# A fused attention and feed-forward kernel: the third tile of p, divided by its sums ahead, is transposed by DMA in 27 of 36 units, in a new order of all engines' steps

## The chip, the cores and the metric

One Trainium2 chip, one NeuronCore. The metric is the device time of one execution in microseconds. Engines: PE (TensorE, matrix products), DVE (VectorE), ACT (ScalarE), POOL (GpSimd), SP (SyncE, which here issues all transfers) and 16 DMA engines.

## The reference, cut to what matters

Attention with queries pooled in pairs, then two feed-forward layers:

```python
q_pool = q.reshape(B, H, S // 2, 2, D).mean(axis=3)          # B, H, S, D = 4, 8, 1152, 64
scores = np.matmul(q_pool, k.transpose(0, 1, 3, 2)) / np.sqrt(D)
attn = np.exp(scores - np.max(scores, axis=-1, keepdims=True))
attn = attn / (np.sum(attn, axis=-1, keepdims=True) + 1e-09)
x = np.matmul(attn, v)                                       # back to 2304 tokens x 512
h = x @ w_in                                                 # 512 -> 2048
g = np.where(h >= 1, h, np.where(h <= -1, 0.0, (h + 1) ** 2 / 4))
x = g @ w_out                                                # 2048 -> 512
out = np.maximum(np.maximum(x @ w1, x @ w2), x @ w3) @ moe2_w_out   # 512 -> 768 -> 512
```

## The kernel before

Values are split into two f16 parts, a high and a low one, and a product is made of three f16 products (high x high, high x low, low x high). For batch 0 (`WHOLE`) p and v stay f32.

The attention runs in 48 units `(b, i, p)`: batch b of 4, block i of 3 blocks of 192 pooled queries, pair p of 4 pairs of heads. A unit has 2 x 192 rows of p, handled as three tiles of 128 rows x 1152 keys (`who` 0, 1, 2): 128 rows of each head, and a third tile with the last 64 rows of both. The steps of a tile are those of `soft`: the scores on PE (`sc`, L490), the row maximum on DVE (L504), exp with the row's sum on ACT (`pf`, L511), and then `turned`, which brings p into the layout with keys on partitions (`pt`), where it meets v.

- For b > 0, tiles 0 and 1 are split on ACT (`hl` high, L582) and DVE (`hl` low, L584), and one DMA transpose on SP (L587) writes both parts to `pt`. `hl` has three buffers (`hlp`, shared with the same kind of step for k), `pf` two and `pt` two.
- Tile 2 is transposed on PE in nine 128 x 128 squares (`tr`, L560) and leaves PSUM by ACT (high, L568) and DVE (low, L570).
- `shares` (steps `r`) adds a small number to the three row sums on POOL (L521), takes reciprocals on DVE (L523), spreads them on POOL (`rb`, L526), transposes them on PE (L532, L536) and copies them to `R` on ACT (L539, L541).
- `av` makes the product with v on PE (L605) and multiplies it by `R` and a scale on DVE (L619).

The first feed-forward layer runs interleaved with the attention, two `up_step`s (`ph`, L672) and one `down_step` (`py`, L700) to a unit. Its last part, beside the preparation of the second layer's weights (steps `h`, `j`, `Z`), comes after the attention; the second layer (L931 and on) follows.

What sets the order: two tables of step names, `ATTENTION` and `AFTER`, written out by hand. Each name runs its generator on to the next `yield`, and the instructions of every engine stand in its queue in just that order (`manual_schedule`). SP's queue is one of them: loads, transposes and stores are issued in the order of the table, and an instruction that waits holds up those behind it. A step `s42.1` is the next step of unit 42's tile 1; `u`, `y`, `a`, `r`, `q`, `k`, `v` are the steps of up, down, `av`, `shares` and the loads.

Of the kernel before, what the change touches and what calls it, by code (L numbers as in the profile page):

```python
# [7 lines left out]
F32 = mybir.dt.float32  # L8
# [15 lines left out]
OWN_BANK = (True, False)  # L24
FOLD = False
RELU = ()
ATTENTION = """
w0 w1 v0 q0 v3 v1 v2 w0 q2 w0 k0 w0 k1 w1 v0 w1 w3 w1 q0 w0 v0 q0 v3 v0 w2 q0 w1 v3 q0 v3 v1 w0 q0 w1 v1 q2 q0
v1 w0 w1 q4 k0 w0 v2 k0 k0 k1 v2 e0 k0 v2 q2 k1 q2 w3 k1 q2 k0 k1 w3 k0 e1 w2 w3 q4 q0 w2 w3 w4 w2 k3 q4 s0.0 k1
w2 w6 s0.1 s0.0 k1 w4 s0.1 s0.0 k2 w4 s0.1 s0.0 w4 k3 s0.1 s0.0 k3 w2 w5 s0.1 s0.2 k3 q2 k3 w3 q4 s1.0 q2 s0.2  # L30
w2 e4 q6 e5 k2 e3 s1.0 q4 s0.2 k2 w3 s1.0 s0.2 r0 k2 r0 k2 q2 w4 w2 s1.0 s0.2 k3 e2 r0 s1.0 s1.1 q6 k2 k3 w6
s1.2 s1.1 w5 r0 a0 r0 k2 w5 s1.1 w6 q6 w6 k5 k4 s1.1 a0 w6 w7 s1.2 s1.1 w5 s1.2 s1.2 r1 r1 w5 o2 q4 r1 s2.0 q6
q4 s1.2 w4 e6 r1 q6 s2.0 q8 w4 s2.1 e7 w5 w4 a1 s2.0 s2.1 w7 w5 q4 s2.1 s2.0 q8 w7 r1 w7 s2.1 s2.0 q8 s2.2 s2.1
a1 w7 s2.2 s3.0 wi w6 s2.2 s3.0 w6 r2 r2 q6 s3.0 r2 w6 q10 s2.2 w7 wi s3.0 s2.2 o0 w7 r2 o1 s3.0 s3.1 q10 q8 r2
s3.2 o2 s3.1 e8 q8 wi q6 e9 s3.2 a2 s3.1 o0 wi q8 s3.2 o2 q12 o2 s3.1 o1 r3 q6 q10 s3.2 s3.1 a2 q12 o4 r3 s3.2
o0 s4.0 r3 o0 o2 s4.1 r3 a3 r3 s4.0 o0 o3 s4.1 s4.0 o1 s4.0 s4.1 a3 s4.0 x0 s4.1 o1 s4.1 s4.2 x0 s5.0 x0 o1 s5.0
u0.0 o3 o4 s4.2 u0.1 s5.0 o4 s4.2 o4 u0.0 s5.0 r4 u0.1 s4.2 s5.0 r4 o5 u0.0 r4 u0.2 s4.2 u0.1 o3 u0.0 s5.1 u0.1
u0.0 o4 q10 s5.2 s5.1 e10 u0.2 r4 q10 q8 a4 r4 s5.2 s5.1 q10 s5.2 o3 q14 s5.1 q12 r5 s5.2 e11 s5.1 q8 u0.3 a4
s5.2 r5 u0.1 r5 u0.2 o5 q14 s6.0 q12 o3 o5 s6.1 q12 u0.2 s6.0 a5 u0.3 s6.1 s6.0 o5 s6.0 s6.1 r5 s6.0 s6.1 u0.3
r5 o6 s6.2 s6.1 a5 u0.2 u0.4 u0.3 s6.2 o5 s7.0 u0.3 u0.4 q12 s6.2 u0.5 s7.0 q16 o6 r6 r6 s6.2 u0.4 s7.0 r6 r6 o6  # L40
# [110 lines left out]
def body(ctx: ExitStack, tc: tile.TileContext, q, k, v, w_in, w_out, w1, w2, w3, w_o2, out):  # L151
    nc = tc.nc
# [1038 lines left out]
```

## Time and profile before

| what | us |
|---|---|
| median of 3 runs | 1109.54 (1108.31 to 1110.57) |
| the profiled execution | 1107.21 |
| its span, first to last instruction | 1105.4 |
| PE busy in the span | 1044.4 (94%) |
| DVE busy | 867.3 (78%) |
| ACT busy | 782.1 (71%) |
| POOL busy | 199.1 (18%) |
| DMA, share of 16 engines | 53.6% |

The shares of the whole span are means over parts of different kinds. Up to about 240 us batch 0 is worked on, beside loads of weights; from there to about 745 us the batches b > 0, with the first feed-forward layer beside them; then the rest of both layers. A tile's transfer is seen in two places: the time that SP is held by issuing it, and the time from issue to landing. The DMA share of a stretch is the mean over 16 engines of the time that packets took, and it can pass 1 where packets overlap.

### The profile page before, as it was taken

The numbers are of one execution on the slowest core, as the hardware profiler recorded it, in microseconds if no ns is written. First come the engines' busy times: TensorE is split into PE (matmuls) and PEld (weight loads), VectorE is DVE, ScalarE is ACT, GpSimd is POOL, SyncE is SP. The second block draws the span as 40 slices with busy tenths as digits, with TensorE's granted clock in tenths as the row PEclk, the third lists the DMA queues.
The fourth block names the chain that finished last, engine by engine and source line by source line (L and its number), as shares of the span: only waits on it lengthen the run. The fifth ranks groups of instructions, "written<-read, shape, count | busy, mean of one in ns | idle before, by whom it ended". The sixth has DMA issues, their size and how long they took to land.

```text
span 1105.4 us, 26924 instructions
## 1 busy us (share of the span) xinstructions
PE 1044.4 (94%) x11127; PEld 868.4 (79%) x11127; DVE 867.3 (78%) x1422; ACT 782.1 (71%) x1402; POOL 199.1 (18%) x257
## 2 busy tenths in 40 slices
PE   1668999999999999999999999999999999999998
PEld 1456877788888888888888888899998877767774
DVE  6999988998879899888999887768957867364341
ACT  6788989988879887888898887866764442353332
POOL 3412213412122222212232210000000116000000
PEclk9899999999999999999999999999999999999999
DMA  9965426687669887676896767446333100100001
GB/s 334 253 183 183 120 53 129 130 183 123 123 121 184 166 174 139 133 138 134 171 208 128 136 107 109 94 104 210 130 126 105 43 11 20 63 20 20 20 16 51
DMA packets 274442, 135.31 MB, mean 122 GB/s; under 512 B 229136, under 2 KB 257552, under 8 KB 273296
## 3 DMA queue, kind: packets, MB, share of 16 engines
q1 hardware_dynamic: 274320, 133.59, 53.6%
q8 instruction: 87, 1.43, 0.5%
q14 instruction: 35, 0.29, 0.1%
HBM read 62.39 MB, written 9.83 MB: 65 GB/s over the span
## 4 chain that ended last, share of the span: by engine, by line
PE 78%; DVE 7%; ACT 6%; DMA 5%; issue 3%; SPq 1%; POOL 0%; DVEq 0%; ACTq 0%; POOLq 0%
PE py L700 17%; PE ph L672 14%; PE p L931 10%; PE sc L490 9%; PE av L605 7%; PE po L1094 6%; PE tr L560 5%; PE pa L1029 4%; PE pb L1029 2%; PE av L600 2%; ACT pf L511 2%; DVE st L504 2%; DMA qn<-in_q_dram 2%; PE pc L1029 1%; DMA vn<-in_v_dram 1%
## 5 line engine op out<-in xcount | busy, mean ns | idle before, releaser
L700 PE MATMUL py<-g,wou 128*128 128x192 f16 x2496 | 213.3, 246 | 1.0 <-ACT t L676 0.9
L504 DVE TENSOR_REDUCE st<-sc 128x1 f32<-128x1152 f32 x144 | 194.3, 1351 | 18.9 <-PE sc L490 18.2
L700 PEld LDWEIGHTS <-wou 128*128 128x128 f16 x2496 | 207.1, 98 | 2.1 <-issue 1.4
L672 PE MATMUL ph<-xh,win 128*128 128x192 f16 x2304 | 204.2, 246 | 1.1 <-ACT t L676 0.5
L672 PEld LDWEIGHTS <-win 128*128 128x128 f16 x2304 | 189.8, 98 | 10.9 <-issue 6.9
L511 ACT ACTIVATE pf<-sc,st,esc 128x1152 f32<-128x1152 f32 x144 | 188.8, 1311 | 6.7 <-DVE st L506 1.7
L490 PE MATMUL sc<-kst,qst 128*64 128x512 f16 (+3 forms) x1152 | 165.9, 329 | 13.2 <-DMA kst<-kpre 7.1
L490 PEld LDWEIGHTS <-qst 128*64 128x64 f16 (+1 forms) x1152 | 79.3, 104 | 72.2 <-issue 18.8
L931 PE MATMUL p<-yh,wm 128*128 128x288 f16 x864 | 107.1, 286 | 0.0
L560 PE MATMUL tr<-ident,pf 128*128 128x128 f32 x648 | 88.8, 287 | 15.4 <-ACT pf L511 15.1
L584 DVE TENSOR_TENSOR hl<-pf,hl 128x1152 f16<-128x1152 f32 x72 | 99.2, 1379 | 3.6 <-ACT hl L582 3.3
L931 PEld LDWEIGHTS <-wm 128*128 128x128 f16 x864 | 84.5, 98 | 21.9
L560 PEld LDWEIGHTS tr<-ident,pf 128*128 128x128 f32 x648 | 75.7, 148 | 22.9 <-ACT pf L511 16.5
L605 PE MATMUL av<-pt,vhl 128*64 128x192 f16 x1944 | 86.9, 247 | 0.4 <-DMA pt<-hl 0.3
L582 ACT ACTIVATE hl<-pf 128x1152 f16<-128x1152 f32 x72 | 83.6, 1161 | 1.2
L605 PEld LDWEIGHTS <-vhl 128*64 128x64 f16 x1944 | 79.6, 110 | 6.2 <-issue 3.2
L676 ACT ACTIVATE t<-ph,Uv 128x384 f32<-128x384 f32 x96 | 55.0, 575 | 26.6 <-PE ph L672 25.7
L1094 PE MATMUL po<-wo,h 128*128 128x512 f16 (+1 forms) x342 | 72.3, 368 | 0.0
L521 POOL TENSOR_SCALAR sm<-sm 128x3 f32<-128x3 f32 x48 | 19.6, 408 | 286.5 <-ACT pf L511 272.0
L570 DVE TENSOR_TENSOR pt<-tr,pt 128x1152 f16<-128x1152 f32 x36 | 48.8, 1355 | 23.0 <-ACT pt L568 22.8
L682 DVE SCALAR_TENSOR_TENSOR t<-t 128x384 f32<-128x384 f32 x96 | 59.0, 615 | 3.3
L686 DVE SCALAR_TENSOR_TENSOR g<-t,dgs,g 128x384 f16<-128x384 f32 x96 | 60.0, 632 | 1.8 <-ACT g L684 1.6
(212 smaller groups left out, 1537.1 us busy)
## 6 DMA issues: line engine op xcount, KB each, us to landing
vn<-in_v_dram SPq DMA_DIRECT2D x16, 576.0 KB, 5.0
kn<-in_k_dram SPq DMA_DIRECT2D x16, 576.0 KB, 4.6
raw_m<-in_moe_w_dram SPq DMA_DIRECT2D x12, 768.0 KB, 4.7
raw_in<-in_moe_w_in_dram SPq DMA_DIRECT2D x8, 1024.0 KB, 7.0
qn<-in_q_dram SPq DMA_DIRECT2D x24, 256.0 KB, 4.1
raw_ou<-in_moe_w_out_dram SPq DMA_DIRECT2D x10, 512.0 KB, 4.1
y_d<-ys SPq DMA_DIRECT2D x52, 96.0 KB, 2.0
qst<-qst SPq DMA_DIRECT2D x48, 96.0 KB, 2.2
```

What stands on the lines that cost most here:

```text
L490: nc.tensor.matmul(sc[m0:m1, n0:n1], qst[b, i, p][who][:, var, m0:m1], ks[:, h, n0:n1], start=(var == 0), stop=(var == 1))
L504: nc.vector.tensor_reduce(out=m, in_=sc, axis=AX.X, op=ALU.max, negate=True)
L511: nc.scalar.activation(out=pf, in_=sc, func=AF.Exp, bias=nb, scale=e, accum_out=sums[b, i, p][:, who:who + 1])
L560: nc.tensor.transpose(tr[:, c * P:(c + 1) * P], pf[:, c * P:(c + 1) * P], ident)
L582: nc.scalar.activation(out=hl[:, 0], in_=pf, func=AF.Copy)
L584: nc.vector.tensor_tensor(out=hl[:, 1], in0=pf, in1=hl[:, 0], op=ALU.subtract)
L605: nc.tensor.matmul(acc[64 * h:64 * h + 64], vhl[b, p][:, vi, h, c, :], pt[:, h, pi * KT + c, :], start=(c == 0 and e == 0), stop=(c == KT ...
L672: nc.tensor.matmul(ph[:, a], win[:, wi, kt, ff * P:(ff + 1) * P], x[:, xi, kt], start=(kt == 0 and e == 0), stop=(kt == KD - 1 and e == 2))
L700: nc.tensor.matmul(py, wou[:, ff // 2, wi, ff % 2, m * P:(m + 1) * P], g[:, gi, ff, :], start=(ff == 0 and e == 0), stop=(ff == NF - 1 and ...
L931: nc.tensor.matmul(ph[:, :NB2], wm[:, wi, i, kt, ff * P:(ff + 1) * P], yh[:, yi, kt, n0:n0 + NB2], start=(kt == 0 and e == 0), stop=(kt == ...
L1029: nc.tensor.matmul(ps[:, :NB2], w(wi, kt), x[:, xi, kt], start=(first and kt == 0 and e == 0), stop=(kt == 1 and e == 2), skip_group_check ...
L1094: nc.tensor.matmul(po, hh[:, hi, ff, t * P:(t + 1) * P], wo[:, wi, ff, c0:c1], start=(n == 0 and e == 0), stop=(n == NF2 - 1 and e == 2))
```

## The change

Three things are changed together.

1. In 27 units with b > 0 (`UNITS`: 13 to 20, 25 to 32 and 37 to 47) all three tiles go by DMA. Each tile's own sums are finished ahead of its split: a small step on POOL, a reciprocal on DVE, and then the high part is made by ACT with the reciprocal as its scale and the low part by DVE with it as its scalar. These units have no `shares`, no `R` and no multiplication by it: the product with v leaves PSUM by a scaled copy on ACT. The other nine units with b > 0 keep the transposes on PE for tile 2, and `shares` makes one transpose more.
2. `pt` has a new layout for b > 0, in which the three tiles stand side by side (tile 0, tile 2, tile 1), so that both heads' 192 columns are adjacent. For the second head the rows of tile 2 are now its first 64, and its q loads are cut accordingly: four transfers for a step `q` with b > 0 instead of three.
3. Both tables are new; 2282 names become 2326 in `ATTENTION`, 182 become 165 in `AFTER`. Three up steps and one down step that stood in `AFTER` now stand in `ATTENTION`. `OWN_BANK` and `FOLD` go, and with them two constants.

```diff
-OWN_BANK = (True, False)
-FOLD = False
+BY_DMA = lambda b, i, p: 12 * b + 4 * i + p in UNITS
+UNITS = (13, 14, 15, 16, 17, 18, 19, 20, 25, 26, 27, 28, 29, 30, 31, 32, 37, 38, 39, 40, 41, 42, 43, 44, 45, 46, 47)
 ATTENTION = """
...
-u10.2 a47
+u10.2 u10.3 u10.2 u10.3 u10.3 u10.3 u10.4 y9.1 y9.1 a47 u10.4 u10.4 u10.4 u10.5 a47
...
     def q_steps(b, i, p):
...
+        shift = 0 if WHOLE(b, p) else P
+        for h in range(2 if shift else 1):
+            hs, r = (slice(h0 + h, h0 + 4, 2), r0 + h * shift) if shift else (slice(h0, h0 + 4), r0)
+            load_q.dma_start(out=qn[:, h:4:2 if shift else 1].rearrange("p a r d -> p a (r d)"),
+                             in_=q[b, hs, r:r + 2 * P].rearrange("h (p r) d -> p h (r d)", r=2))
...
     def shares(b, i, p):
...
+        nc.tensor.transpose(rs[:, 0:P], rb.rearrange("p a o -> p (a o)"), ident)
+        nc.tensor.transpose(rs[:, P:2 * P], third, ident)
+        if not WHOLE(b, p):
+            nc.tensor.transpose(rs[:, 2 * P:3 * P], rb.rearrange("p a o -> p (a o)"), ident)
...
     def turned(b, i, p, who, pf):
...
+        at_ = slice(*((0, P), (2 * P, 3 * P), (P, 2 * P))[who])
+        if who == 2 and not BY_DMA(b, i, p):
...
         hl = hlp.tile([P, 2, KT * P], F16, tag="hl", name=f"hl{key}")
-        nc.scalar.activation(out=hl[:, 0], in_=pf, func=AF.Copy)
-        yield
-        nc.vector.tensor_tensor(out=hl[:, 1], in0=pf, in1=hl[:, 0], op=ALU.subtract)
-        yield
-        pt = new_pt(b, i, p)
-        nc.sync.dma_start_transpose(out=pt[:, who, :, 0:P], in_=hl.rearrange("p a b -> p (a b)"))
+        if BY_DMA(b, i, p):
+            share = sums[b, i, p][:, who:who + 1]
+            nc.gpsimd.tensor_scalar(out=share, in0=share, scalar1=1e-9 * 2.0 ** 12, scalar2=2.0 ** -15, op0=ALU.add,
+                                    op1=ALU.mult)
+            yield
+            nc.vector.reciprocal(out=share, in_=share)
+            yield
+            nc.scalar.activation(out=hl[:, 0], in_=pf, func=AF.Copy, scale=share)
+            yield
+            nc.vector.scalar_tensor_tensor(out=hl[:, 1], in0=pf, scalar=share, in1=hl[:, 0], op0=ALU.mult,
+                                           op1=ALU.subtract)
+        else:
+            nc.scalar.activation(out=hl[:, 0], in_=pf, func=AF.Copy)
+            yield
+            nc.vector.tensor_tensor(out=hl[:, 1], in0=pf, in1=hl[:, 0], op=ALU.subtract)
+        yield
+        nc.sync.dma_start_transpose(out=new_pt(b, i, p)[:, :, at_], in_=hl.rearrange("p a b -> p (a b)"))
...
     def av(b, i, p):
...
+        if not BY_DMA(b, i, p):
+            nc.vector.scalar_tensor_tensor(out=xf[b, i][:, p, :], in0=acc, scalar=Uv[b][:, p:p + 1],
+                                           in1=R.pop((b, i, p)), op0=ALU.mult, op1=ALU.mult)
+        else:
+            nc.scalar.activation(out=xf[b, i][:, p, :], in_=acc, func=AF.Copy, scale=Uv[b][:, p:p + 1])
```

Where steps stand now, in three places. In the rows, a name like `sc3_1_3_1` is the tile of unit (b, i, p) = (3, 1, 3) and tile 1, and the last number counts buffers.

PE, the 44th unit, before: behind the first scores come the nine transposes of the unit ahead, then a down step, and ahead of the products with v (`av`) the two transposes of the reciprocals.

```order
L490 MATMUL sc3_1_3_0_10402<-kst3_3_8318,qst3_1_2_9753 128x128
...
L672 MATMUL ph2_2_7_10414<-xh2_2_8945,win_73 128x192
...
L560 MATMUL tr3_1_2_2_10445<-ident_80,pf3_1_2_2_10411 128x128 x9
...
L700 MATMUL py2_1_3_10464<-g2_1_8513,wou_74 128x192
...
L490 MATMUL sc3_1_3_1_10520<-kst3_3_8318,qst3_1_2_9753 128x128
L532 MATMUL tr3_1_2_2_10445<-ident_80,rb3_1_2_10462 128x128
L536 MATMUL tr3_1_2_2_10445<-ident_80,sm3_1_2_10194 128x128
...
L605 MATMUL av3_1_2_10533<-pt_3_1_2_10320,vhl3_2_9074 64x192
```

The same place now:

```order
L492 MATMUL sc3_1_3_0_10255<-kst3_3_8585,qst3_1_2_9474 128x512
...
L695 MATMUL ph3_0_1_10268<-xh3_0_9951,win_73 128x192
...
L629 MATMUL av3_1_1_10302<-pt_3_1_1_10086,vhl3_1_8740 64x192
...
L492 MATMUL sc3_1_3_1_10366<-kst3_3_8585,qst3_1_2_9474 128x512
...
L726 MATMUL py2_2_0_10380<-g2_2_9322,wou_74 128x192
...
L492 MATMUL sc3_1_3_2_10442<-kst3_3_8585,qst3_1_2_9474 64x512
```

The transposes are gone, and the products with v that stand beside the scores of unit (3, 1, 3) are those of (3, 1, 1), one unit later than before.

SP, the transfers of units (3, 1, 1) and (3, 1, 2), before: two to a unit.

```order
L587 DMA_TRANSPOSE pt_3_1_1_10098<-hl3_1_1_0_10011 128x18x128
L462 DMA_TRANSPOSE qst3_2_0_10146<-qpre3_2_0_9536 128x6x128
...
L587 DMA_TRANSPOSE pt_3_1_1_10098<-hl3_1_1_1_10150 128x18x128
L707 DMA y_d2_68<-ys2_1_2_10282 128x192
L587 DMA_TRANSPOSE pt_3_1_2_10320<-hl3_1_2_0_10272 128x18x128
L587 DMA_TRANSPOSE pt_3_1_2_10320<-hl3_1_2_1_10398 128x18x128
L707 DMA y_d2_68<-ys2_1_3_10528 128x192
```

Now:

```order
L601 DMA_TRANSPOSE pt_3_1_1_10086<-hl3_1_1_0_9947 128x18x128
L601 DMA_TRANSPOSE pt_3_1_1_10086<-hl3_1_1_1_10008 128x18x128
L601 DMA_TRANSPOSE pt_3_1_1_10086<-hl3_1_1_2_10135 128x18x128
L601 DMA_TRANSPOSE pt_3_1_2_10263<-hl3_1_2_0_10194 128x18x128
L733 DMA y_d2_68<-ys2_1_3_10248 128x192
L601 DMA_TRANSPOSE pt_3_1_2_10263<-hl3_1_2_1_10251 128x18x128
L601 DMA_TRANSPOSE pt_3_1_2_10263<-hl3_1_2_2_10357 128x18x128
```

Each unit has a third transfer, and the store of y stands between two of them.

POOL, around unit (1, 0, 3), before: the sums of all three tiles are one step (`sm`, 128x3).

```order
L521 TENSOR_SCALAR sm1_0_3_3030<-sm1_0_3_3030 128x3
L526 COPY rb1_0_3_3312<-sm1_0_3_3030 128x128
L449 TENSOR_TENSOR qn2_0_2_3370<-qn2_0_2_3370 128x6x64
L521 TENSOR_SCALAR sm1_1_0_3289<-sm1_1_0_3289 128x3
L374 TENSOR_SCALAR xh1_0_3560<-xf1_0_2961,Uv1_2962 128x768
```

Now:

```order
L587 TENSOR_SCALAR sm1_0_3_3082<-sm1_0_3_3082 128x1
L451 TENSOR_TENSOR qn1_2_2_3157<-qn1_2_2_3157 128x6x64
L587 TENSOR_SCALAR sm1_0_3_3082<-sm1_0_3_3082 128x1
L451 TENSOR_TENSOR qn2_0_2_3192<-qn2_0_2_3192 128x6x64
L587 TENSOR_SCALAR sm1_0_3_3082<-sm1_0_3_3082 128x1
L587 TENSOR_SCALAR sm1_1_0_3286<-sm1_1_0_3286 128x1 x3
```

Each tile has its own step on POOL, and additions of q (`qn`), which wait for a load, stand between the steps of one unit.

## Rows read from the trace of the kernel before

**Rows 1.** Windows of the whole core over five stretches of b > 0, columns named first.

```profile
core 0: us, PE busy (x) PEld busy (x) DVE busy (x) ACT busy (x) POOL busy (x), PEclk, DMA share, GB/s
228.00:342.82 114.82, 114.24 (x1451) 100.63 (x1452) 99.30 (x152) 95.16 (x177) 24.84 (x37) 1.00 0.72 135
342.82:421.59 78.77, 77.81 (x975) 67.83 (x976) 73.05 (x103) 66.92 (x126) 17.39 (x23) 1.00 0.88 172
421.59:536.99 115.40, 114.03 (x1455) 100.63 (x1452) 101.34 (x156) 97.45 (x180) 24.12 (x39) 1.00 0.76 147
536.99:597.96 60.97, 60.00 (x754) 52.65 (x754) 58.47 (x86) 53.66 (x99) 20.50 (x21) 1.00 0.85 170
597.96:741.46 143.50, 143.32 (x1839) 127.18 (x1839) 117.29 (x167) 114.70 (x209) 15.79 (x33) 1.00 0.60 107
```

**Rows 2.** Timeline of PE, 714 to 729 us: start, duration, engine, line, work.

```profile
714.40 2.42 PE L605 MATMUL av<-pt,vhl 128*64 128x192 f16 x54
...
722.67 1.15 PE L560 MATMUL tr<-ident,pf 128*128 128x128 f32 x9
723.66 4.12 PE L700 MATMUL py<-g,wou 128*128 128x192 f16 x48
...
728.59 0.28 PE L532 MATMUL tr<-ident,rb 128*128 128x128 f32 x1
...
728.91 2.42 PE L605 MATMUL av<-pt,vhl 128*64 128x192 f16 x54
```

**Rows 3.** Groups by line: busy us, mean ns of one, then idle before it.

```profile
L619 DVE SCALAR_TENSOR_TENSOR xf<-av,Uv,R 128x192 f32<-128x192 f32 x48 | 19.9, 415 | 13.1 <-PE av L605 9.9 <-PE av L600 1.3 <-ACT R L541 0.4
L570 DVE TENSOR_TENSOR pt<-tr,pt 128x1152 f16<-128x1152 f32 x36 | 48.8, 1355 | 23.0 <-ACT pt L568 22.8
L376 DVE SCALAR_TENSOR_TENSOR vhl<-vn,sb,vhl 128x1152 f16<-128x1152 f32 x12 | 17.0, 1414 | 1.0 <-POOL vhl L374 1.0
L523 DVE RECIPROCAL sm<-sm 128x3 f32<-128x3 f32 x48 | 8.0, 167 | 2.2 <-POOL sm L521 1.6
L568 ACT ACTIVATE pt<-tr 128x1152 f16<-128x1152 f32 x36 | 40.4, 1122 | 3.8 <-PE tr L560 3.8
L582 ACT ACTIVATE hl<-pf 128x1152 f16<-128x1152 f32 x72 | 83.6, 1161 | 1.2
L539 ACT ACTIVATE R<-tr 128x192 f32<-128x192 f32 x36 | 11.8, 329 | 5.4 <-PE tr L536 5.4
L541 ACT ACTIVATE R<-tr 64x64 f32<-64x64 f32 x36 | 7.9, 219 | 1.1
L704 ACT ACTIVATE ys<-py,yd 128x192 f32<-128x192 f32 x52 | 21.7, 418 | 28.2 <-PE py L700 26.6 <-ACT g L684 1.3
```

**Rows 4.** Who waited for whom, in total, times, longest: POOL's additions of q.

```profile
POOL qn L449 <- DMA qn<-in_q_dram: 95.2, 20, 10.1
```

**Rows 5.** One transfer alone (a window), then all 72 of them on SP.

```profile
735.00:740.00 5.00, 5.00 (x61) 4.99 (x59) 3.54 (x8) 3.66 (x7) 0.59 (x2) 1.00 0.64 118
...
L587 SPq DMA_TRANSPOSE pt<-hl x72: 2339/2796/5830, 217.1 to 735.0; - x72
...
DMA to landing us min/median/max: 4.6/5.0/7.9
```

**Rows 6.** Windows with the highest DMA shares, columns as in Rows 1.

```profile
0.00:50.00 50.00, 16.32 (x78) 11.94 (x79) 39.62 (x76) 35.23 (x53) 16.99 (x26) 0.94 1.01 308
340.00:370.00 30.00, 29.34 (x366) 25.18 (x364) 27.97 (x37) 26.66 (x49) 4.30 (x7) 1.00 1.08 199
```

**Rows 7.** Timeline around the start of the second layer, columns as in Rows 2.

```profile
815.45 3.00 DVE L876 SCALAR_TENSOR_TENSOR yh<-yf,ysc,yh 128x576 f16<-128x576 f32 x4
...
831.13 4.08 PE L931 MATMUL p<-yh,wm 128*128 128x288 f16 x32
```

**Rows 8.** Timeline of one tile from its high part to the issue of its transfer.

```profile
446.25 1.17 ACT L582 ACTIVATE hl<-pf 128x1152 f16<-128x1152 f32 x1
...
450.90 3.40 SPq L587 DMA_TRANSPOSE pt<-hl  x1
```

More of the change, by code (lines that the diff above doesn't have):

```diff
@@ L31 @@
[L31 to L40, printed above, removed]
@@ L227, in body @@
                             channel_multiplier=1)
-    halves = const.tile([P, P], F32, name="halves")
-    fold = const.tile([P, 64], F32, name="fold")
-    nc.gpsimd.memset(halves, 0.0)
-    for h in range(2):
-        nc.gpsimd.memset(halves[64 * h:64 * h + 64, 64 * h:64 * h + 64], 1.0)
-    nc.gpsimd.tensor_tensor(out=fold, in0=ident[:, 0:64], in1=ident[:, 64:P], op=ALU.add)
     ones16 = const.tile([P, 32], BF16, name="ones16")
@@ L561, in turned @@
             yield
-            if who == 2 and not OWN_BANK[b > 0]:
-                R[b, i, p] = rs
-            pt = new_pt(b, i, p)
-            if not WHOLE(b, p):
-                tr = tr.rearrange("p (c h q) -> p h c q", c=KT, h=2)
-                hi, lo = pt[:, :, 0:KT, P:NB], pt[:, :, KT:2 * KT, P:NB]
-                nc.scalar.activation(out=hi, in_=tr, func=AF.Copy)
-                yield
-                nc.vector.tensor_tensor(out=lo, in0=tr, in1=hi, op=ALU.subtract)
-                yield
-                return
-            pt = whole(pt)
+            pt = whole(new_pt(b, i, p))
             if who < 2:
@@ L580, in turned @@
             return
-        hl = hlp.tile([P, 2, KT * P], F16, tag="hl", name=f"hl{key}")
-        nc.scalar.activation(out=hl[:, 0], in_=pf, func=AF.Copy)
+        at_ = slice(*((0, P), (2 * P, 3 * P), (P, 2 * P))[who])
+        if who == 2 and not BY_DMA(b, i, p):
+            tr = place(f"tr{key}")[:, :KT * P]
+            for c in range(KT):
+                nc.tensor.transpose(tr[:, c * P:(c + 1) * P], pf[:, c * P:(c + 1) * P], ident)
+            yield
+            pt, tr = new_pt(b, i, p), tr.rearrange("p (c q) -> p c q", c=KT)
+            hi, lo = pt[:, 0:KT, at_], pt[:, KT:2 * KT, at_]
+            nc.scalar.activation(out=hi, in_=tr, func=AF.Copy)
+            yield
+            nc.vector.tensor_tensor(out=lo, in0=tr, in1=hi, op=ALU.subtract)
+            yield
+            return
@@ L679, in up_step @@
         yield
-        if NBL * b + i not in RELU:
+        if NBL * b + i in ON_POOL:
+            nc.gpsimd.tensor_scalar(out=t2, in0=t2, scalar1=1.0, scalar2=0.0, op0=ALU.add, op1=ALU.max)
+            yield
+        elif NBL * b + i not in RELU:
             nc.vector.tensor_scalar(out=t2, in0=t2, scalar1=1.0, scalar2=0.0, op0=ALU.add, op1=ALU.max)
```

276 lines of the change are left out of this document (144 added, 132 removed).

## The prediction

> **What bounds the kernel now.** I read the windows first, cut at five places of the batches b > 0 [rows 1]. In all five TensorE (PE) is busy for nearly the whole stretch: 114.24 of 114.82 us, 77.81 of 78.77, 114.03 of 115.40, 60.00 of 60.97, 143.32 of 143.50, so 509.4 of 513.5 us with 4.1 us idle. [...] VectorE (DVE) has 449.4 us of work there (87.5%), ScalarE (ACT) 427.9 us (83%), and the DMA engines stand at shares of 0.72, 0.88, 0.76, 0.85 and 0.60, which is 82.7 + 69.3 + 87.7 + 51.8 + 86.1 = 377.6 us. So PE sets the end of this part and three others stand close behind it. What shortens PE's row of work shortens the kernel, until one of those three is reached. The second thing to see is how PE's idle share moves with DVE's share over the five stretches: 0.1% idle at 82% (last row), 0.5% at 86% (first), 1.2% at 88% and at 93% (third and second), 1.6% at 96% (fourth).
>
> The 27 units lie in the first, third and fifth stretch (8 + 8 + 11). The second and fourth are where k and v of the next batch are loaded, and there the third tile stays on PE.
>
> **The change, part by part.**
>
> *PE, removed.* In steady state a unit's products with v begin 728.91 - 714.40 = 14.51 us after those of the unit before [rows 2]. Of this the nine transposes of the third tile hold PE from 722.67 to the start of the next work at 723.66, 0.99 us, and the two transposes of the reciprocals from 728.59 to 728.91, 0.32 us. Both go in 27 units: 27 x 1.31 = 35.4 us. The nine units left over get a third transpose of reciprocals, 9 x 0.11 us (0.99 / 9) = 1.0 us. Net **-34.4 us**, all of it on the path, since PE waits for nothing there. A unit should then take 13.2 us.
>
> *DVE.* Out of PSUM the third tile's low part took 1355 ns (L570). It becomes an operation with a scalar per row, as do the other two tiles' low parts; the nearest row for that form at this size is the split of v, 1414 ns [rows 3]. So 3 x 0.06 = 0.18 us more, two reciprocals more at 0.167 us (0.33), and the multiplication L619 at 0.415 us less: about +0.10 us a unit, **+2.6 us** of work in all, beside PE.
>
> *ACT.* The third copy becomes one out of SBUF (1161 ns for 1122), the two copies of the reciprocals go (329 + 219 ns), and the output product moves here from DVE, for which I take the like copy L704, 418 ns [rows 3]. That is -0.09 us a unit, about -2.4 us in 27. Its place is hidden under PE as before.
>
> *GpSimd (POOL).* One operation on three sums and one copy become three small ones, which now stand between a tile's exponential and its high part. That is an added wait, on POOL's own queue: in 11 places of the new order a q addition stands one or two rows ahead of such a share step, and those additions wait for loads of q, 95.2 us in 20 waits now [rows 4]. Queued behind are the reciprocal, the high part, the low part and the transfer. As the loads are issued well ahead and a tile has most of a unit before it is used, I take 0; if each of the 11 cost the mean wait of 4.8 us it would be 53 us, and that end is kept for the slow side.
>
> *SyncE (SP) and DMA.* 27 transfers more. One alone fills the window 735 to 740 at 0.64, so it takes 5 x 0.64 = 3.2 us of all engines; SP is held 2.8 us by each, and it lands 5.0 us (up to 7.9) after its issue [rows 5]. On SP three of them are 8.4 us of a 13.2 us unit; behind them stand the stores of y and the loads of q, of which 18 are now cut in two for the same bytes. On the DMA engines each stretch gets 3.2 us a unit:
>
> first: 82.7 + 8 x 3.2 = 108.3 us of DMA, against 114.24 - 8 x 1.31 = 103.8 us of PE;
> third: 87.7 + 25.6 = 113.3 against 103.6;
> fifth: 86.1 + 35.2 = 121.3 against 128.9.
>
> The measure can go over 1: it stood at 1.08 for 30 us and at 1.01 over the first 50 us [rows 6]. With 1.08 as what can be had, the first stretch is not bound (100.3) and the third gives back 1.3 us (104.9). With 1.01 they take 107.2 and 112.2, which gives back 3.4 + 8.6 = 12 us. DVE's share rises to 452 / 479 = 94%, where PE's idle should be about 1.5% instead of 0.8%, 3 us more. The two causes overlap, so the give-back lies between 3 and 12; I take **10 us**, nearer to the 1.01, since 50 us is closer to the length of these stretches than 30.
>
> [...]
>
> The new order also moves the products with v one unit later on PE (those of 3_1_1 now stand where those of 3_1_2 stood), which leaves a transfer more room than the 5 us it needs; but pt still has two buffers, so a unit's first transfer now stands on SP until the products of two units before are done, and I cost that at nothing as long as PE keeps its pace.
>
> *After the attention.* The text of the new order lets three up steps and one down step fewer stand behind the last unit, so PE has less to do while the second layer's weights are made ready. Before, the last part of the input was ready at 818.45 (815.45 + 3.00) and PE first used it at 831.13 [rows 7]: 12.7 us of cover. I cost it at nothing; by the down step of 4.1 us and three up steps of half that (two up steps have as many products as one down step), some 10 us of the cover go. If it were gone, the excess would stand in front of L931.
>
> *Sum.* The profiled execution took 1107.21 us with a span of 1105.4. 1107.2 - 34.4 + 10 = 1082.8; the median of the runs lies 2.3 us above that execution, so **1085 us**.
>
> **The rivals.**
>
> *The full gain.* Give-back of 3 us or none, and perhaps part of the old idle goes too: 1107.2 - 34.4 + 2.3 = 1075, within 1066 to 1079. For it: the measure reached 1.08, and DVE ran at 96% with PE at 98% in the fourth stretch. Against it: both at once, for 100 us, is nowhere in the trace.
>
> *DMA bound.* If 0.95 is what these engines give beside SP's in-order issue, the stretches take 108.3 / 0.95 = 114 and 113.3 / 0.95 = 119 us, which gives back 10 + 16 = 26 us: 1101, band 1093 to 1107. For it: the first 50 us were mostly plain loads, which moved 308 GB/s at 1.01, where a transfer moves 184 at a full share. Against it: 1.08 over 30 us had transposes in it.
>
> *Nothing gained.* DVE really paces and PE only fills: then 452 us of it at today's 87.5% take 516 us, 3 more than now, 1112. Against it: the fourth stretch at 96%.
>
> *Slower: the ring of three hl buffers.* Each DMA tile holds one from the start of its high part until the transfer has landed. In the trace that is from 446.25 to 450.90 + 5.0, 9.65 us [rows 5, 8]. With three tiles a unit, three buffers come round once a unit, so the unit can't be shorter than the time that one is held: harmless up to 13.2 us, no gain left from 14.5 us, slower beyond. If each transfer stood behind one issue of the worst length seen, 5.83 us, it would be 15.5 us, 27 x 1.0 us slower than now: 1136, band 1112 to 1136. For it: DMA and SP are both far busier than now, and POOL's queue stands in the same chain. Against it: 5 us are missing to the deciding point, and the old maximum of landing takes only 2.9 of them.
>
> [...]
>
> **How the numbers follow.** Forecast, 1079 to 1093: 0.45. Full gain, 1066 to 1079: 0.20, of which 0.03 below 1068. DMA bound, 1093 to 1107: 0.17. No change to within 0.2% (about what a measurement of this kernel can tell), 1107 to 1112: 0.05. Slower: 0.13, from 1112 up. So faster 0.82, same 0.05, slower 0.13. From 1068 to 1108 is left out 0.03 below and 0.17 above.
>
> **What would show it.** In the new trace the transposes of tiles should count 9 x 9 for b > 0 and 27 x 9 fewer in all; products with v should follow each other by about 13.2 us in the last units. If the give-back is DMA's, the first and third stretch stand at shares of 1.0 or more and PE waits for pt, or ACT's high part for hl. If DVE's, PE's idle time is spread over the sc and ph rows with DVE above 95%. The forecast is wrong if PE idles more than 25 us between the first and the last product with v out of pt, if landing takes much over 8 us, or if POOL's share steps wait for q loads and ACT's high part waits for the reciprocal. A start (b = 0) that moved by more than 5 us would be a cause that this sum does not hold.

## The result and the profile after

The changed kernel takes 1096.63 us (median of 4 runs, 1095.34 to 1098.93) against 1108.92 us of the kernel before in the same session (1107.32 to 1110.57): a ratio of 0.9888, 95% interval 0.9873 to 0.9903, so 12.3 us less. The forecast was 1085 within 1068 to 1108: the direction and the range held, the size of the gain was half of the 24.5 us (1109.54 - 1085) forecast. The profiled execution has a span of 1095.3 us, against 1105.4 before.

The windows of the changed kernel, cut at the same products with v as [rows 1], but for the first cut: here it is the first product of unit 12, at 241.05 us, which stood at 239.97 us before, while [rows 1] begin at 228.00. The columns are those of [rows 1]: length, busy time and instructions of PE, PE's weight loads, DVE, ACT and POOL, then granted clock, DMA share and GB/s.

```profile
241.05:354.25 113.20, 108.73 (x1398) 93.87 (x1394) 100.84 (x155) 96.67 (x173) 24.34 (x37) 1.00 0.94 175
354.25:429.05 74.80, 70.68 (x893) 61.34 (x892) 66.92 (x106) 61.59 (x115) 20.76 (x33) 1.00 0.96 183
429.05:543.57 114.52, 108.23 (x1348) 91.39 (x1347) 99.38 (x152) 96.28 (x172) 23.16 (x37) 0.98 0.94 171
543.57:608.01 64.44, 63.14 (x784) 55.38 (x783) 55.36 (x92) 51.49 (x95) 21.19 (x28) 0.99 0.93 179
608.01:741.24 133.23, 132.96 (x1736) 115.83 (x1736) 113.84 (x171) 112.59 (x199) 15.79 (x37) 1.00 0.86 154
```

Read them against [rows 1]. The fifth stretch (units 37 to 47) is now 133.2 us long, PE stands still for 0.3 us of it, and its share of DMA rose from 0.60 to 0.86: the change does there most of what it should, 10.3 us in ten units. In the other four the DMA share is 0.93 to 0.96, and PE, which stood still for 0.6 to 1.4 us in each before, now does so for 4.5, 4.1, 6.3 and 1.3 us. Over all five that is 16.5 us; before, with the first stretch cut at 239.97, it was 3.5 us (501.49 us with 498.00 of PE).

Whom PE waited for between 240 and 745 us in the changed kernel (microseconds in all, times, longest):

```profile
PE av L629 <- DMA pt<-hl: 3.9, 4, 2.1
PE sc L492 <- ACT pf L513: 3.3, 4, 1.7
PE tr L575 <- ACT pf L513: 3.1, 3, 1.7
PE sc L492 <- DVE pt L581: 2.7, 1, 2.7
PE ph L695 <- ACT py L731: 1.7, 2, 1.4
```

The products with v wait for a transfer, and the scores and the transposes that are left wait for an exponential. So two kinds of cause are in question: transfers that come late, and a chain on ACT and DVE that comes late. The two lines of tile transposes that are left (PE busy us, mean ns, then idle time before it) show that the edit is whole, 81 of them for b > 0 where there were 324:

```profile
L561 PE MATMUL tr<-ident,pf 128*128 128x128 f32 x324 | 44.6, 292 | 17.2 <-ACT pf L513 17.0
L575 PE MATMUL tr<-ident,pf 128*128 128x128 f32 x81 | 11.7, 294 | 3.1 <-ACT pf L513 3.1
```

### The profile page after: what moved, and what is told of

Same layout as the page of the kernel before. It is cut to its first block, busy times and chain, and to the rows that moved or that the text cites. A ratio compares the mean times of both kernels' runs of the same rounds, so it can differ in the third digit from the quotient of the medians.

```text
span 1095.3 us, 26457 instructions
## 1 busy us (share of the span) xinstructions
PE 1019.0 (93%) x10839; PEld 836.7 (76%) x10839; DVE 860.6 (79%) x1449; ACT 779.5 (71%) x1375; POOL 211.3 (19%) x280
## 3 DMA queue, kind: packets, MB, share of 16 engines
q8 instruction: 85, 1.39, 0.5%
## 4 chain that ended last, share of the span: by engine, by line
PE 70%; DVE 11%; DMA 6%; ACT 6%; issue 3%; POOL 1%; SPq 0%; ACTq 0%; DVEq 0%; POOLq 0%
PE py L726 15%; PE ph L695 13%; PE p L957 10%; PE sc L492 8%; PE po L1120 6%; PE av L629 6%; PE pa L1055 5%; DMA pt<-hl 3%; DVE st L506 3%; ACT pf L513 2%; PE pb L1055 2%; PE av L624 1%; PE tr L561 1%; PE pc L1055 1%; DVE hl L594 1%
## 5 line engine op out<-in xcount | busy, mean ns | idle before, releaser
L594 DVE SCALAR_TENSOR_TENSOR hl<-pf,sm,hl 128x1152 f16<-128x1152 f32 x81 | 116.2, 1440 | 8.3 <-ACT hl L592 8.0
L592 ACT ACTIVATE hl<-pf,sm 128x1152 f16<-128x1152 f32 x81 | 100.8, 1248 | 10.0 <-issue 3.3
L629 PEld LDWEIGHTS <-vhl 128*64 128x64 f16 x1944 | 80.2, 110 | 11.5 <-issue 6.8
L587 POOL TENSOR_SCALAR sm<-sm 128x1 f32<-128x1 f32 x81 | 30.5, 376 | 235.7 <-ACT pf L513 233.4
L710 ACT ACTIVATE g<-t,dgs 128x384 f16<-128x384 f32 x96 | 57.7, 607 | 9.6 <-DVE t L708 9.3
L561 PE MATMUL tr<-ident,pf 128*128 128x128 f32 x324 | 44.6, 292 | 17.2 <-ACT pf L513 17.0
L1120 PEld LDWEIGHTS <-h 128*128 128x128 f16 x342 | 33.5, 98 | 34.1
L708 DVE SCALAR_TENSOR_TENSOR t<-t 128x384 f32<-128x384 f32 x96 | 56.4, 588 | 3.3
```

What stands on the lines that cost most here:

```text
L592: nc.scalar.activation(out=hl[:, 0], in_=pf, func=AF.Copy, scale=share)
L594: nc.vector.scalar_tensor_tensor(out=hl[:, 1], in0=pf, scalar=share, in1=hl[:, 0], op0=ALU.mult, op1=ALU.subtract)
L629: nc.tensor.matmul(acc[64 * h:64 * h + 64], vhl[b, p][:, vi, h, c, :], pt[:, pi * KT + c, h * NB:h * NB + NB], start=(c == 0 and e == 0), ...
L1120: nc.tensor.matmul(po, hh[:, hi, ff, t * P:(t + 1) * P], wo[:, wi, ff, c0:c1], start=(n == 0 and e == 0), stop=(n == NF2 - 1 and e == 2))
```

## The theories and the experiments

Forecast were 34.4 us off PE and 10 us of them given back. Measured are 12.3 us, so 22.1 us were given back. Where? **Theory 1:** the DMA engines have no more to give in units 13 to 32, where loads of q, k and v still run beside them; units 37 to 47 bring their whole gain. **Theory 2:** the new chain from the exponential over POOL's step, the reciprocal and ACT's high part delays each tile, and the rings of hl and pf pass that on. **Theory 3:** the new order has thin places. All times below are medians; ratios are to the kernel before, run beside each.

### One part of the units alone

*The changed code, no third tile by DMA, the old tables.*

```diff
-UNITS = (13, ..., 20, 25, ..., 32, 37, ..., 47)
+UNITS = ()
 ATTENTION, AFTER = those of the kernel before
```

> The changed code with the tables of before and no unit whose third tile goes by DMA; what is left of the change is the transpose of the third reciprocal and the rearranged loads of q. All theories: within 4 us of before, 1105 to 1110 us. A gain of over 4 us would mean that part of the 12 us does not come from the third tiles at all.

Measured: 1116.46 us, ratio 1.0060 (1.0045 to 1.0075). All theories missed this: the code costs 6.7 us by itself. It is taken up below; for the next two runs it is the base, and in this code a unit on PE has three transposes of reciprocals, so that one unit sent by DMA should be worth 1.31 + 0.11 = 1.42 us. (The last section of runs corrects this price: the third transpose could not be found, and a PSUM bank was.)

*Units 37 to 47 alone.*

```diff
-UNITS = (13, ..., 20, 25, ..., 32, 37, ..., 47)
+UNITS = (37, ..., 47)
 ATTENTION = order of before up to the first step of s37.0, then the order of the changed kernel
```

> Order of before up to the first step of unit 37, then the order of the changed kernel; only units 37 to 47 (no loads of k and v beside them) send their third tile by DMA. PE loses 11 x 1.31 = 14.4 us. Theory 1 (DMA engines full beside the loads, so units 13 to 32 gave everything back): 1092 to 1097 us, at least as fast as the changed kernel with its 27 units. Theory 2 (the share steps and the small rings delay the exponentials in every such unit): 1098 to 1104 us. Theory 3 (the new order in the non-DMA units costs): 1090 to 1096 us.

Measured: 1101.19 us, ratio 0.9921 (0.9906 to 0.9936). From 1.0060 that is 1.39%, 15.4 us, where 11 x 1.42 = 15.6 was to be had. So little or nothing is given back in these units, neither to DMA nor to the share steps. As it stands the time lies in theory 2's range (1098 to 1104); all three ranges were written without the code's own loss of 6.7 us, of which the 25 units left on PE still carry the greater part. Part of the 15.4 us is the bank that these units no longer use; the pair of runs without it is at the end of the experiments.

*Units 13 to 20 and 25 to 32 alone.*

```diff
-UNITS = (13, ..., 20, 25, ..., 32, 37, ..., 47)
+UNITS = (13, ..., 20, 25, ..., 32)
 ATTENTION = order of the changed kernel up to the first step of s36.2, then the order of before
```

> The complement: order of the changed kernel up to unit 36, then that of before; only units 13 to 20 and 25 to 32 send their third tile by DMA. PE loses 16 x 1.31 = 21 us. Theory 1: nothing is gained, 1105 to 1112 us. Theory 2: a third of it is gained as everywhere, 1100 to 1104 us. Theory 3: 1108 to 1114 us, slower than before.

Measured: 1114.31 us, ratio 1.0046 (1.0029 to 1.0063). From 1.0060 that is 1.6 us of 16 x 1.42 = 22.7. So these 16 units gave back some 21 us (to within some 2.5), nearly all, and they are where nearly the whole error of the forecast lies. As it stands the time lies a little above all three ranges; less the code's 6.7 us it would be 1107.6, in theory 1's. This run doesn't tell theory 1 from theory 3, since the order of these units is new as well. Since the share steps are the same in both groups of units, theory 2 has little ground left unless the loads make it worse.

### Half the bytes

```diff
-nc.sync.dma_start_transpose(out=new_pt(b, i, p)[:, :, at_], in_=hl.rearrange("p a b -> p (a b)"))
+nc.sync.dma_start_transpose(out=new_pt(b, i, p)[:, 0:KT, at_], in_=hl[:, 0])
 ...
-pt[:, pi * KT + c, h * NB:h * NB + NB]
+pt[:, c, h * NB:h * NB + NB]
```

> The changed kernel, but every transfer turns the high halves alone (half the bytes), and the product with the low halves of p reads the high halves instead, so PE does as much as in the changed kernel and the result leaves the low halves of p out of the units after the first batch. Theory 1 (DMA engines full): the idle time of PE between 240 and 600 us falls from some 16 us to under 5, 1083 to 1088 us, near the forecast of 1085. Theory 2 (share steps and rings): 1094 to 1098 us, no change against the changed kernel. Theory 3 (order): the same, 1094 to 1098 us.

Measured: 1085.46 us, ratio 0.9784 (0.9768 to 0.9799), 1.04% or 11.5 us below the changed kernel. (That this is the forecast time is a coincidence: the run also halves the transfers of the first two tiles.) The windows of this run, cut at the same products; the counts of PE's instructions are those of the changed kernel to one, so the lengths can be compared as they stand:

```profile
238.99:348.04 109.05, 108.36 (x1397) 93.71 (x1393) 100.93 (x155) 96.53 (x173) 25.96 (x37) 1.00 0.65 122
348.04:421.07 73.03, 70.44 (x893) 61.40 (x892) 66.99 (x106) 61.89 (x115) 20.87 (x33) 1.00 0.74 146
421.07:531.46 110.39, 105.51 (x1348) 89.63 (x1347) 98.94 (x152) 95.22 (x171) 22.39 (x36) 1.00 0.61 115
531.46:595.75 64.29, 63.95 (x784) 56.33 (x783) 58.31 (x94) 52.15 (x98) 21.94 (x30) 0.97 0.74 143
595.75:728.65 132.90, 132.90 (x1736) 115.76 (x1735) 112.51 (x169) 112.76 (x199) 15.06 (x36) 1.00 0.51 83
```

The gain is 4.2, 1.8 and 4.1 us in the first three stretches and 0.2 and 0.3 us in the last two (2.1 us more stand ahead of the first cut; three runs of the changed code in the order of before reach that product at 239.87, 240.87 and 240.93 us, 1.1 us apart): it sits where the 16 units are (and in the four between them, where k and v of the next batch are loaded), and in the last stretch, where the DMA share falls from 0.86 to 0.51, it is nearly nothing. Not all of it is waiting: in the third stretch PE's idle time falls by 1.4 us and its busy time, with the same instructions, by 2.7, at a granted clock of 1.00 instead of 0.98. And PE's idle time fell to 8.5 us, not under 5 as theory 1 expected. The wait of the products with v is gone:

```profile
PE tr L575 <- ACT pf L513: 3.3, 3, 1.7
PE sc L492 <- DVE pt L581: 2.7, 1, 2.7
PE sc L492 <- ACT pf L513: 1.9, 4, 0.9
PE rs L533 <- DVE ub L190: 0.3, 1, 0.3
```

Three things change together in this run. The line of the transfers (min, median and max ns for which one holds SP) and the time from issue to landing, first of the changed kernel, then of this one:

```profile
L601 SPq DMA_TRANSPOSE pt<-hl x99: 2488/2837/6591, 213.0 to 734.7; - x99
...
DMA to landing us min/median/max: 4.5/5.0/8.6
```

```profile
L601 SPq DMA_TRANSPOSE pt<-hl x99: 1242/1307/4164, 208.3 to 720.3; - x99
...
DMA to landing us min/median/max: 3.2/3.3/8.2
```

Half a transfer also holds SP for about half the time (1.31 us for 2.84). Added up from the rows of SP's timeline, issuing held it for 293 of the 340 us from 240 to 580 in the changed kernel (86%), against 231 us before and 193 us with half the bytes. And a transfer of the high half alone reads only what ACT wrote, so it no longer has to wait for DVE's low part (1.44 us). So "the transfers" means the engines' share, SP's time, the earlier start, or several of them; no run here changed one without the others. The share alone doesn't settle it either: 0.94 is a mean and not a ceiling, since the changed kernel itself held 1.12, with 209 GB/s, for 20 us:

```profile
520.00:540.00 20.00, 17.13 (x196) 13.93 (x193) 17.55 (x21) 16.88 (x30) 4.11 (x4) 0.95 1.12 209
```

*The same in units 13 to 20 and 25 to 32 alone* (the edit above on the run with these 16 units).

> Units 13 to 20 and 25 to 32 alone by DMA in the changed order, as in the run that gave 1114.3 us, but every transfer turns the high halves alone (half the bytes; the low halves of p are left out of the result and the high ones multiplied in their place). Theory 1 (these 16 units gave their gain back to the DMA engines): half or more of the 20.5 us given back returns, 1099 to 1105 us. If the order or the share steps took it: 1111 to 1115 us.

Measured: 1103.39 us, ratio 0.9943 (0.9924 to 0.9962), from 1.0046 that is 1.03%, 11.4 us. The same 11.5 us as in the full kernel: all that the halved bytes return, they return in these 16 units. It is half of the 21 us given back there. What else?

### The chain and the rings

```diff
+even = const.tile([P, 1], F32, name="even")
+nc.vector.memset(even, 2.0 ** -22)
-nc.scalar.activation(out=hl[:, 0], in_=pf, func=AF.Copy, scale=share)
+nc.scalar.activation(out=hl[:, 0], in_=pf, func=AF.Copy, scale=even)
-nc.vector.scalar_tensor_tensor(out=hl[:, 1], in0=pf, scalar=share, in1=hl[:, 0], op0=ALU.mult,
+nc.vector.scalar_tensor_tensor(out=hl[:, 1], in0=pf, scalar=even, in1=hl[:, 0], op0=ALU.mult,
```

> The changed kernel, but the tiles that go by DMA are multiplied by a constant instead of their share: POOL's step and the reciprocal still run, yet neither the high nor the low part waits for them (the division of these tiles is left out of the result). Theory 1 (transfers): within 2 us of the changed kernel, 1095 to 1098 us. Theory 2 (the chain of POOL, DVE and ACT that now stands ahead of each high part): 1085 to 1091 us.

Measured: 1096.70 us, ratio 0.9869 (0.9838 to 0.9900), against 0.9888 of the changed kernel: 0.2% less, within the two intervals, which leave room for a gain of up to some 6 us. The edit frees ACT's high part. On DVE the reciprocal still stands ahead of the low part and still waits for POOL, though for little (240 to 745 us; 3.1 us in the changed kernel):

```profile
DVE sm L592 <- POOL sm L589: 2.2, 4, 1.3
```

So theory 2 finds no support, and neither does the fear of 11 additions of q ahead of share steps.

```diff
-hlp = at.enter_context(tc.tile_pool(name="hlp", bufs=3, side="right"))
+hlp = at.enter_context(tc.tile_pool(name="hlp", bufs=4, side="right"))
```

> The changed kernel with four hl buffers instead of three. Theory 1 (the DMA engines have no more to give between 260 and 580 us): the high part no longer waits for a transfer to land, but the products with v still do; 1094 to 1097 us. Theory of the ring (my rival of three buffers): the waits of the high part for DMA, 4.7 us in all in this stretch, and what hangs on them go, 1087 to 1092 us.

Measured: 1096.39 us, ratio 0.9869 (0.9853 to 0.9885), again 0.2% less and within the intervals. The high parts' waits for a transfer, 2.4 + 2.3 us in the changed kernel, are gone from ACT's list. In their place the high parts wait 3.4 us for the reciprocal instead of 1.2, and the products with v wait a little more for transfers (4.9 us instead of 3.9):

```profile
PE av L629 <- DMA pt<-hl: 4.9, 6, 1.9
PE sc L492 <- ACT pf L513: 4.2, 5, 1.9
PE sc L492 <- DVE pt L581: 2.7, 1, 2.7
```

So the ring of three was mainly a place where late transfers showed, not what made them late.

### The order

In the changed kernel PE stands still at the first unit that turns its third tile on PE again (unit 33), in both of the runs with half the bytes too. PE's timeline there (start, duration, line, work, and in brackets the wait before it):

```profile
531.85 1.20 PE L575 MATMUL tr<-ident,pf 128*128 128x128 f32 x9
532.89 1.14 PE L492 MATMUL sc<-kst,qst 128*128 128x512 f16 x6
536.74 2.98 PE L492 MATMUL sc<-kst,qst 128*64 128x512 f16 x18 [2.71 <-DVE pt L581]
...
541.46 2.18 PE L575 MATMUL tr<-ident,pf 128*128 128x128 f32 x9 [0.87 <-ACT pf L513]
```

Two score products follow each other with no up or down step between, and the second wants the PSUM bank that DVE's low part still reads. After that wait the granted clock fell: windows of 5 us, columns as above.

```profile
530.00:535.00 5.00, 4.03 (x62) 3.18 (x57) 2.65 (x5) 4.97 (x10) 0.83 (x2) 1.00 1.27 278
535.00:540.00 5.00, 3.26 (x21) 1.76 (x22) 4.97 (x6) 4.55 (x8) 0.00 (x0) 0.81 1.03 198
540.00:545.00 5.00, 4.13 (x33) 3.71 (x33) 4.45 (x8) 4.52 (x8) 3.30 (x3) 0.51 1.00 184
```

At 0.51 the nine transposes at 541.46 last 2.18 us, where those at 531.85 lasted 1.20. I moved a down step of 4.1 us from unit 34 into the gap:

```diff
-... s34.1 s34.0 s34.2 u6.7 ... v12 r33 s34.2 ... r34 y5.3 k13 ... s35.2 y5.3 k14 v15 s35.2 y5.3 ...
+... s34.1 s34.0 y5.3 s34.2 u6.7 ... v12 y5.3 y5.3 r33 s34.2 ... r34 k13 ... s35.2 k14 v15 s35.2 ...
```

> The changed kernel with one down step (4.1 us of PE) moved from unit 34 to unit 33, between two score products where PE idled 2.7 and 0.9 us at 534 to 541 us and its granted clock then fell to 0.81 and 0.51. Theory 3 (a thin place in the new order, with the clock that falls after it, is part of the loss): 1090 to 1094 us and a clock of 1.00 there. If ACT and DVE set the pace there, the idle time only moves: 1095 to 1098 us.

Measured: 1099.81 us, ratio 0.9901 (0.9877 to 0.9925), no gain (the time is a little above both ranges). The gap is filled, but the wait now stands 20 us further on; the two windows of this run:

```profile
520.00:540.00 20.00, 19.88 (x245) 17.22 (x245) 16.53 (x19) 17.30 (x30) 4.07 (x4) 1.00 1.12 212
540.00:560.00 20.00, 12.82 (x159) 9.63 (x159) 16.67 (x28) 15.83 (x31) 7.36 (x9) 1.00 0.85 177
```

PE lost 4.1 us in these 40 us in the changed kernel and 7.3 here; the clock stays at 1.00, and the time is no better. One step moved by hand doesn't mend the place. Since 3.2 us more of waiting came in place of the clock's fall, the run gives no price for the fall by itself; an estimate from the changed kernel's windows is 0.05 x 17.13 us of PE from 520 to 540 (clock 0.95) and 0.12 x 18.79 from 540 to 560 (0.88), 3.1 us in all if PE's work follows the clock. Theory 3 is neither shown nor out.

```diff
-UNITS = (13, ..., 20, 25, ..., 32, 37, ..., 47)
+UNITS = (13, 15, 17, 19, 25, 27, 29, 31, 37, ..., 47)
 ATTENTION = changed order; in the other eight units the third tile's PE transposes stand ahead
             of its high part, the reciprocals' transposes ahead of the products with v
```

> The changed kernel with every second unit of 13 to 32 (14, 16, 18, 20, 26, 28, 30, 32) turned on PE again, with the rest of the order kept. PE gets 8 x 1.42 = 11.4 us back. Theory 1: the DMA share between 260 and 580 us falls from 0.97 to about 0.87, the 20.5 us given back by the first 16 units mostly go, 1086 to 1093 us, faster than the changed kernel although it does more on PE. Otherwise 1100 to 1108 us.

Measured: 1130.34 us, ratio 1.0170 (1.0151 to 1.0188), far from both. PE's longest waits between 240 and 620 us are others than before:

```profile
PE sc L492 <- DVE pt L581: 12.6, 6, 3.3
PE tr L575 <- ACT pf L513: 8.9, 7, 2.8
PE av L629 <- ACT R L544: 5.5, 7, 0.9
PE sc L492 <- ACT pf L513: 2.1, 4, 0.9
PE av L629 <- DMA pt<-hl: 0.6, 1, 0.6
```

The DMA share from 260 to 580 us fell from 0.97 to 0.77 and the wait for transfers from 3.9 to 0.6 us, as theory 1 says, but a third tile put back on PE takes one of the two score banks in an order that was written without it, and that costs far more. The run says nothing on theory 1's price, and much on how closely the order fits its units.

### What the code costs by itself

```diff
-rs = psg.tile([P, 512], F32, tag="g1", name=f"rs{b}_{i}_{p}")[:, :3 * P]
+rs = the columns 1152 to 1535 of the tile's own bank tr, where b > 0
```

> As the run with the changed code, the tables of before and no third tile by DMA (1116.5 us), but the reciprocals are transposed into the spare columns of the tile's own PSUM bank again, not into one of the two small banks that the products with v also use. If the shared small banks cost the 2.7 us that 36 transposes of 0.11 us do not explain: 1113 to 1114.5 us. If not: 1116 to 1118 us.

Measured: 1111.42 us, ratio 1.0007 (0.9997 to 1.0016); from 1.0060 that is 5.9 us, to within some 2 us. In the kernel before, the transposed reciprocals of b > 0 lay in the spare columns of the tile's bank (they are written to tr, [rows 2]); the changed code gives them one of the two small banks that the products with v, the up and the down steps take turns in. The windows 240 to 600 us, first without, then with the edit:

```profile
240.00:600.00 360.00, 354.07 (x4489) 311.60 (x4487) 319.29 (x476) 302.41 (x556) 81.02 (x115) 1.00 0.77 151
```

```profile
240.00:600.00 360.00, 357.06 (x4526) 314.06 (x4525) 319.42 (x478) 305.00 (x557) 82.87 (x115) 1.00 0.77 150
```

PE's idle time in the same stretch falls from 5.9 to 2.9 us, and 37 more of its instructions fit in. The edit overshot the expectation: the bank is nearly the whole 6.7 us.

```diff
 (on top of the edit above)
-nc.tensor.transpose(rs[:, 2 * P:3 * P], rb.rearrange("p a o -> p (a o)"), ident)
-nc.scalar.activation(out=r[64:P], in_=rs[64:P, NB:3 * P], func=AF.Copy)
+nc.scalar.activation(out=r[64:P, 0:64], in_=rs[64:P, NB:2 * P], func=AF.Copy)
+nc.scalar.activation(out=r[64:P, 64:NB], in_=rs[64:P, 0:P], func=AF.Copy)
```

> As the run before this one, and with two transposes of reciprocals instead of three in every unit, the result read out by three copies on ACT instead of two. If the third transpose holds PE 0.11 us in each of 36 units: 4.0 us less than the run before this one, and within 0.2% of the kernel before when the bank was the rest, 1108 to 1112 us. If the code loss lies elsewhere (the loads of q cut in two, the start): 1112 to 1114 us.

Measured: 1111.38 us, ratio 1.0006 (0.9993 to 1.0019). One transpose fewer and one copy more in 36 units come to nothing; the 4.0 us expected for the transpose did not appear.

*Units 37 to 47 alone, with both edits.*

> Units 37 to 47 by DMA in the changed order, the rest in the order of before, and in the units that stay on PE the own bank and two transposes. By the sums so far: 1101.2 less what the two edits return on 25 of 36 units (2.5 to 4.5 us), 1096 to 1099 us, about the changed kernel's time with 16 third tiles fewer by DMA; under 1094 us it would beat it.

Measured: 1097.79 us, ratio 0.9882 (0.9868 to 0.9897), as fast as the changed kernel (0.9888, 0.9873 to 0.9903). So the other 16 units in their new order are worth about as much as the bank costs the changed kernel (1.5 us in its nine units on PE, an estimate from 5.9 x 9 / 36): without them, and with the bank put right, the time is the same. The changed kernel with the bank put right, which might beat both, was not run.

This run also gives the cleanest price of a unit, since against the run before it (1.0006) neither bank nor third transpose differs: 1.24%, 13.8 us for 11 units, 1.25 us each, where 11 x 1.31 = 14.4 us were forecast. The 15.4 us above hold, besides, the bank's cost in 11 of 36 units (5.9 x 11 / 36 = 1.8 us, an estimate).

## Why the prediction was right in sign and half right in size

- **PE.** 1.31 us a unit was nearly right: the cleanest pair of runs gave 1.25 in units 37 to 47. The windows give less. Ten units of the last stretch took 143.50 us before and 133.23 now, so 1.03 a unit, with PE waiting for 0.3 us. (There are 24 more products of up steps in it, 44.52 for 42.79 us of PE, and 18 fewer of scores, 29.77 for 31.97 us, which nearly cancel.) The forecast of 13.2 us started from one unit of 14.51 us, and the mean unit there was 14.35; so the 13.3 measured hits it partly by luck. Some of the time that the transposes left went to other products: from start to start a product with v takes 43.6 ns there (42.0 before) and one of the down step 83.8 (82.5 before). Why is not shown. The 9 x 0.11 us for third transposes could not be found (1.0006 against 1.0007).
- **The give-back: the term that was mis-sized.** Taken were 10 us within 3 to 12; measured are 22.1. The amount of DMA work was sized well: 0.94 x 113.20 = 106 us and 0.94 x 114.52 = 108 us in the first and third stretch, forecast 108.3 and 113.3. What failed is the step that took 1.01 from [rows 6] as the share that a whole stretch can hold, "since 50 us is closer to the length of these stretches than 30". That row is mostly of plain loads at the start (31 of the 35 transfers issued in it; 4 are transposes). With three transposes to a unit the stretches ran at 0.94 and 0.94, with PE waiting, though single windows of 20 us reached 1.12. So the sign that the prediction named for this cause, shares of 1.0 or more, did not appear as written. The 0.94 is near the 0.95 of the rival "DMA bound", whose band of 1093 to 1107 holds the result; its 26 us were somewhat too many. With the transfers halved 11.5 of the 22.1 us came back, in two kernels, but SP's time and the wait for the low part went with the bytes, so which of the three it was stays open. The trace of before shows the two kinds apart: one transposing transfer alone had 118 GB/s at a share of 0.64 [rows 5], about 184 at a full one (118 / 0.64, an estimate), against 308 at 1.01 in the first 50 us [rows 6]; in the first and third stretch of the changed kernel 175 and 171 GB/s went with a share of 0.94.
- **DVE's part of the give-back,** 3 us for a share of 94% over the five stretches, had no ground: the share measured there is 87% (436.33 of 500.19 us).
- **The rest of the give-back** is 10.6 us. With half the bytes PE still stands idle for 8.5 us over the five stretches (0.7, 2.6, 4.9, 0.3, 0.0), 5.0 more than the kernel before in the stretches cut alike; its longest waits there are for ACT's exponential and DVE's low part, and 2.7 us of them stand at unit 33, a place of the new order. The bank, a cost that the sum did not hold, should make 5.9 x 9 / 36 = 1.5 us in the nine units still on PE (an estimate; it wasn't run in the changed kernel). The granted clock of 0.97 in that run's fourth stretch may be 0.03 x 63.95 = 1.9 us (an estimate, if PE's work follows the clock), and the dearer products named under PE are a part as well. These overlap in an unknown degree, and no run separates them: the rest stays open.
- **DVE.** +2.6 us was forecast beside PE; in the whole program its busy time fell from 867.3 to 860.6 us. The split with a scalar per row takes 1440 ns (taken: 1414).
- **ACT.** -2.4 us was forecast, 782.1 to 779.5 was measured; but one price was wrong. The high part was taken at 1161 ns [rows 3] and with a scale per row it takes 1248, 81 x 0.087 = 7 us that the sum did not hold. Other groups of ACT fell by as much, and in the last stretch PE waited for only 0.3 us in all.

```profile
L594 DVE SCALAR_TENSOR_TENSOR hl<-pf,sm,hl 128x1152 f16<-128x1152 f32 x81 | 116.2, 1440 | 8.3 <-ACT hl L592 8.0
L592 ACT ACTIVATE hl<-pf,sm 128x1152 f16<-128x1152 f32 x81 | 100.8, 1248 | 10.0 <-issue 3.3 <-DMA pt<-hl 2.3 <-DVE sm L590 1.2
```

- **POOL's added wait, taken as 0.** Right as far as the runs tell: with ACT not waiting for it the time is the same within the intervals (0.9869 against 0.9888), and the reciprocal's wait for POOL is 3.1 us in all.
- **The ring of three hl buffers,** the rival on the slow side, did not decide: a fourth buffer took off 0.2%, within the intervals. The ring of two `pt` buffers, whose wait on SP the prediction took as nothing, was not tested; SP is without a transfer to issue for only 47 of the 340 us from 240 to 580, so this wait and all its others fit in that.
- **After the attention.** Forecast: some 10 us less cover of 12.7, and no cost. The input is ready at 811.93 + 3.00 = 814.93 and first used at 820.99; 6.1 us are left, and PE doesn't wait:

```profile
811.93 3.00 DVE L902 SCALAR_TENSOR_TENSOR yh<-yf,ysc,yh 128x576 f16<-128x576 f32 x4
```

```profile
820.99 14.25 PE L957 MATMUL p<-yh,wm 128*128 128x288 f16 x115
```

- **The start** was forecast to stay. PE is busy for 184.9 us of the first 240 (187.2 before). Three runs of the changed code in the order of before have 185.3, 188.4 and 188.4 us there and so differ as much among themselves: this is no term.

## What to carry to other kernels

Moving work from the bounding engine to DMA pays by the stretch: ask in each what share the DMA engines have already and for how much of the time the issuing queue is held, and take what a stretch can hold from rows with the same kind of transfer and of the same length, not from plain loads or short windows. Here eleven units with 0.60 of DMA beside them returned 1.25 of the 1.31 us each, and sixteen with 0.72 and 0.76 returned about nothing (1.6 us in all); halving their transfers brought back about half of it. And run the new code with the move switched off: it showed a cost of 0.6% (a PSUM bank shared with other work) that none of the views of the whole change above names. And change one thing at a time in such a run: halving the bytes here also halved the queue's time and freed the transfers of a wait.

## What was not expected of the hardware

- Half a transposing transfer holds SP for 1.31 us instead of 2.84 (0.46 of it), but lands after 3.3 us instead of 5.0 (0.66 of it; medians).
- The DMA share of the changed kernel is 0.94 over stretches of 113 to 115 us and 1.12 over 20 us of them.
- ACT's copy of 128x1152 from f32 to f16 takes 1161 ns plain and 1248 ns with a scale per row.
- After 2.7 us of waiting PE's clock stood at 0.81 and 0.51 in two windows of 5 us, and nine transposes took 2.18 us instead of 1.20. In the run with the gap filled there the clock stayed at 1.00, and the time was no better.
